# Linear attention and a gated MLP on one core: batch 1's q loaded ahead of its k and transposed by DMA, with two stages reordered around it

## The chip, the core and the metric

The kernel runs on one core of a Trainium2 chip. A core has a tensor engine (PE; its weight loads are listed apart as PEld), a vector engine (VectorE, DVE), a scalar engine (ScalarE, ACT), GpSimd (POOL) and a sync engine (SyncE, SP), which here only issues DMA transfers. All engines run their own lists of instructions in program order and wait for each other by semaphores. The core's 16 DMA engines move all transfers; those issued by GpSimd appear as queue q0 (software_dynamic), those issued by SyncE as queue q1 (hardware_dynamic). SBUF is the on-chip memory with 128 partitions, PSUM the small memory into which the tensor engine writes.

The metric is the device time of one execution in microseconds. Before the change its median is 295.08 us over 3 runs (294.52 to 295.19).

## The reference

Eight batches of eight heads, 576 positions, 64 values a head. Linear attention, then an MLP whose gate has a slope of its own for each of the 2048 inner features:

```python
def _attn_ref(q, k, v):                       # each (8, 8, 576, 64)
    def phi(x):
        return np.where(x > 0, x, np.exp(x) - 1.0) + 1.0
    q_p, k_p = (phi(q), phi(k))
    kv = np.einsum('bhsd,bhse->bhde', k_p, v)
    z = np.sum(k_p, axis=2)
    num = np.einsum('bhsd,bhde->bhse', q_p, kv)
    den = np.einsum('bhsd,bhd->bhs', q_p, z)[..., None] + 1e-06
    return num / den

def _moe_ref(x, w_in, w_out, beta):           # x (4608, 512), w_in (512, 2048), w_out (2048, 512)
    h = x @ w_in
    g = h * (1.0 / (1.0 + np.exp(-beta * h)))
    return g @ w_out
```

Between the two, the heads of a position are laid side by side, so that x has one row of 512 for each of the 4608 positions.

## The kernel before

The program is written in the order in which each engine is to run it; no scheduler moves anything. phi is computed as min(exp(x), max(x, 0) + 1): the exponential `e` on ScalarE, the rest on VectorE.

```python
def phi_all(b, a):                            # a is "q" or "k"; each in two halves pr of four heads
    phi_tile(b, a)
    for pr in range(2):
        phi_part(b, a, pr, xin(b, a, pr))     # e, ScalarE
    for pr in range(2):
        phi_relu(b, a, pr, xin(b, a, pr))     # r, VectorE
    for pr in range(2):
        phi_min(b, a, pr)                     # min(e, r), VectorE
```

The sums over k (`z_products`) and the products of k with v (`kv_direct`) are both chains of 36 small products for each half, with k as the stationary operand. `z_evac` and `kv_evac` bring them to SBUF and mask the parts that belong to other heads.

```python
def row_products(b, pr, dsts, mov):
    for j in range(J):                        # J = 9
        for hh in range(2):
            r = slice(hh * G, (hh + 1) * G)   # G = 64
            nc.tensor.matmul(dsts[hh], st[b, "k"][r, pr, j, :], mov(r, j),
                             start=(j == 0), stop=(j == J - 1), skip_group_check=True)
```

For the denominators (`dens`) and the numerators (`numer`, `numer0`) q must stand with its 64 values on the partitions. There are two ways to that. `q_trans` lets the tensor engine multiply by the identity, into PSUM, and copies from there (18 products and 5 copies a batch). `q_trans_dma` lets two DMA transfers do it, issued by SyncE, each for 64 rows:

```python
def q_trans_dma(b):
    st[b, "qTd"] = work.tile([P, 38, G], BF16, tag="qT", name="qTd")
    nc.gpsimd.memset(st[b, "qTd"][:, 36:37], 0.0)
    for hh in range(2):
        st[b, "qTd", "dma"] = nc.sync.dma_start_transpose(
            out=st[b, "qTd"][:, hh * 2 * J : (hh + 1) * 2 * J],
            in_=st[b, "q"][hh * G : (hh + 1) * G].rearrange("p a j c -> p (a j c)"),
        )

def q_stat(b, t, hh, pr, n):
    if (b, "qTd") in st:
        i = (hh * 2 + pr) * J + 2 * t
        return st[b, "qTd"][:, i : i + 2, :].rearrange("p j g -> p (j g)")
    return st[b, "qT"][:, t, pr, hh, 0:n]
```

Before the change batches 0 and 1 use `q_trans`, batches 2 to 7 `q_trans_dma`. From batch 3 on, the loads of the q and k after that wait until the transposition has landed (`hold`, with the reason "share of the queues").

The loads are issued by GpSimd in this order, and cast f32 to bf16 on the way (w_out alone stays f32):

```python
# k of batch 0, v of batch 0, w_in in four quarters, then
for i in range(3):
    load_w_out(i)
load(nc.gpsimd, xk[1], k, 1)
load(nc.gpsimd, xq[1], q, 1)
load_w_out(3)
load(nc.gpsimd, vb[1], v, 1)
# ... and, written after batch 0's h:
load(nc.gpsimd, xq[2], q, 2)
load(nc.gpsimd, xk[2], k, 2)
load(nc.gpsimd, vb[0], v, 2)
```

The front, batch 0 (`idle` puts products without use on the tensor engine, to keep its clock up):

```python
idle(3)
zt = [num0_tile() for _ in range(2)]
z_products(0, 0, zt)
idle(6)
z_products(0, 1, zt)
bps = miscps.tile([P, FC], F32, tag="misc", name="bps")
nc.tensor.matmul(bps, beta_row, ident16, is_transpose=True, start=True, stop=True)
nc.scalar.copy(beta_s, bps)
z_evac(zt)
# ...
kv_direct(0, 0, kvp0)
for hh in range(2):
    kv_evac(0, hh, (0,), kvp0)
dens(0, range(4), dps)
recips(0, 4, P, dps)
numer_part((0, 1), 0)                         # products and norm on VectorE
numer_part((2, 3), 0)
kv_direct(0, 1, kvp0)
# then x_part (transposes x, copy on ScalarE) and h0_part (pieces of h, first quarter of w_in)
```

Batch 0's y = g @ w_out, in four quarters of the inner features, with batch 1's attention between them. `y_mm(0, t, i, ...)` is four products of 512 columns, row group t, quarter i; `w_out_scale` divides a quarter of w_out by beta on VectorE, four instructions.

```python
for i in range(3):
    w_out_scale(i, 0)
yps = [mm_tile("y_ps") for _ in range(4)]
phi_all(1, "k")
phi_all(1, "q")
for i in range(2):
    for t in range(4):
        y_mm(0, t, i, yps[t])
kv1 = [miscps.tile([P, 512], F32, tag="misc", name="kv1") for _ in range(2)]
kv_tile(1)
y_mm(0, 0, 2, yps[0])
y_mm(0, 1, 2, yps[1])
for pr in range(2):
    z_products(1, pr, kv1)
z_evac(kv1)
w_out_scale(3, 0)
y_mm(0, 2, 2, yps[2])
for ts in ((0, 1), (2, 3)):
    q_trans(1, ts, num0_tile().bitcast(BF16), (nc.scalar, nc.scalar))
y_mm(0, 3, 2, yps[3])
dps1 = num0_tile()
q_trans(1, (4,), dps1.bitcast(BF16)[:, 512:768], (nc.scalar,))
for pr in range(2):
    kv_direct(1, pr, kv1)
for hh in range(2):
    kv_evac(1, hh, (0, 1), kv1)
dens(1, range(NT), dps1)                      # NT = 5
# recips, y_mm(0, 0, 3), numer0(1, 0), numer0(1, 1), then the rest of y, numer0 and x_trans in turn
```

Then follow, for batches 1 to 8 (8 is the remainder of all batches), `h_phase`, 16 steps of four products of 512 columns, and `y_phase`, 16 more, in which the next batches' attention is woven in at numbered steps (`at(sh, step, ...)`, `at(sy, step, ...)`). PSUM has two buffers for the transpositions of x (`miscps`).

Of the kernel before, what the change touches and what calls it, by code (L numbers as in the profile page):

```python
# [9 lines left out]
BF16 = mybir.dt.bfloat16  # L10
# [6 lines left out]
def kernel(  # L17
# [10 lines left out]
    nc = tc.nc  # L28
# [50 lines left out]
    def load(eng, dst, src, b, h0=0, n=4):  # L79

        rows = src[b].rearrange("h (g j) d -> (h g) (j d)", j=J)
        return eng.dma_start(  # L82
            out=dst[:, h0 : h0 + n].rearrange("p h j d -> p h (j d)"),
            in_=rows.rearrange("(i p) e -> p i e", p=P)[:, h0 : h0 + n],
        )
# [34 lines left out]
    def load_w_out(i):  # L120
        nc.gpsimd.dma_start(out=w_out_f[i], in_=w_out_v[:, i * 4 : (i + 1) * 4, :])
# [6 lines left out]
    def idle(n, cols=512):  # L128
        for _ in range(n):
            nc.tensor.matmul(  # L130
                warm_ps[:, 0:cols], warm[:, 0:P], warm[:, 0:cols], start=True, stop=True
            )
# [70 lines left out]
    def kv_direct(b, pr, ps):  # L203
        row_products(
            b, pr, [a[:, pr * P : (pr + 1) * P].rearrange("p (h d) -> p h d", h=2) for a in ps],
            lambda r, j: vb[b][r, 2 * pr : 2 * pr + 2, j, :],
        )

    def kv_evac(b, hh, prs, ps):
        p0, p1 = prs[0], prs[-1] + 1  # L210
        nc.vector.tensor_mul(
            st[b, "kv"][:, hh, p0:p1].rearrange("p a (h e) -> p a h e", h=2)[:, :, :, 0:D],
            ps[hh][:, p0 * P : p1 * P].rearrange("p (a h d) -> p a h d", a=p1 - p0, h=2),
            kvmask[:, p0:p1, :, 0:D],
        )
# [54 lines left out]
# [5 lines that stand above are left out]
# [68 lines left out]
    def mm_tile(name):  # L343
        return mmps.tile([P, 512], F32, tag="mm", name=name)

    def y_mm(b, t, i, yp, c0=0, c1=512):
        for c in range(4):
            ff = 4 * i + c
            nc.tensor.matmul(  # L349
                yp[:, c0:c1],  # L350
                g_sb[b % 2][:, ff, t * P : (t + 1) * P],
                w_out_sb[i][:, c, c0:c1],
                start=(ff == 0), stop=(ff == FC - 1), skip_group_check=True,
            )
# [22 lines left out]
    def phi_all(b, a):  # L377
        phi_tile(b, a)
        for pr in range(2):
            phi_part(b, a, pr, xin(b, a, pr))  # L380
        for pr in range(2):
            phi_relu(b, a, pr, xin(b, a, pr))
        for pr in range(2):
            phi_min(b, a, pr)
# [19 lines left out]
    def dens(b, ts, dps):  # L404

        for t in ts:
            n = P if t < NT - 1 else G
            for hh in range(2):
                for pr in range(2):
                    c = ((t * 2 + hh) * 2 + pr) * 2  # L410
                    nc.tensor.matmul(
                        dps[:n, c : c + 2], q_stat(b, t, hh, pr, n), z0[:, hh, pr, :],
                        start=True, stop=True, skip_group_check=True,
                    )

# [5 lines left out]
    def num0_tile():  # L421
        return num0ps.tile([P, 512], F32, tag="num0", name="nps0")

    def numer0(b, t):
        n = P if t < NT - 1 else G
        nps = num0_tile()
        for hh in range(2):
            for pr in range(2):
                nc.tensor.matmul(  # L429
                    nps[:n, (hh * 2 + pr) * P : (hh * 2 + pr + 1) * P].rearrange(  # L430
                        "p (h d) -> p h d", h=2
                    ),
                    q_stat(b, t, hh, pr, n),
                    st[b, "kv"][:, hh, pr, :].rearrange("p (h e) -> p h e", h=2)[:, :, 0:D],
                    start=True, stop=True, skip_group_check=True,
                )
        norm(b, t, n, nps[:n].rearrange("p (a h d) -> p a h d", a=2, h=4), rden0[:n, t])
# [14 lines left out]
    phi_step("q", 1, phi_relu)  # L452
    for i in range(3):
        load_w_out(i)
    load(nc.gpsimd, xk[1], k, 1)
    load(nc.gpsimd, xq[1], q, 1)
    load_w_out(3)
    load(nc.gpsimd, vb[1], v, 1)
    phi_step("q", 1, phi_min, 0, 4)
# [15 lines left out]
    idle(3)  # L475
    zt = [num0_tile() for _ in range(2)]
    z_products(0, 0, zt)
    idle(6)
    z_products(0, 1, zt)
    bps = miscps.tile([P, FC], F32, tag="misc", name="bps")  # L480
    nc.tensor.matmul(bps, beta_row, ident16, is_transpose=True, start=True, stop=True)
# [4 lines left out]
        q_trans(0, (t,), misc_bf()[:, 0 : 512 if t < NT - 1 else 256], (nc.scalar,))  # L486

    def numer_part(ts, pr):

        nps = num0_tile()  # L490
        for i, t in enumerate(ts):
            for hh in range(2):
                nc.tensor.matmul(  # L493
                    nps[:, (i * 2 + hh) * P : (i * 2 + hh + 1) * P].rearrange(
                        "p (h d) -> p h d", h=2
                    ),
                    q_stat(0, t, hh, pr, P),
                    st[0, "kv"][:, hh, pr, :].rearrange("p (h e) -> p h e", h=2)[:, :, 0:D],
                    start=True, stop=True, skip_group_check=True,
                )  # L500
        for i, t in enumerate(ts):
            if pr == 0:
                st[0, "xs", t] = work.tile([P, 4, 2, D], BF16, tag="xs", name="xs", bufs=4)
            nc.vector.tensor_mul(
                st[0, "xs", t][:, 2 * pr : 2 * pr + 2].rearrange("p i a d -> p a i d"),
                nps[:, i * 256 : (i + 1) * 256].rearrange("p (a h d) -> p a h d", a=2, h=2),
                rden0[:, t, :, 2 * pr : 2 * pr + 2, None].to_broadcast([P, 2, 2, D]),
            )
# [20 lines left out]
                    skip_group_check=True,  # L529
                )  # L530

    kv_direct(0, 0, kvp0)
    for hh in range(2):
        kv_evac(0, hh, (0,), kvp0)
    dens(0, range(4), dps)
    recips(0, 4, P, dps)
    numer_part((0, 1), 0)
    numer_part((2, 3), 0)
    kv_direct(0, 1, kvp0)

# [65 lines left out]
    for i in range(3):  # L606
        w_out_scale(i, 0)
    yps = [mm_tile("y_ps") for _ in range(4)]
    phi_all(1, "k")
    phi_all(1, "q")  # L610
    for i in range(2):
        for t in range(4):
            y_mm(0, t, i, yps[t])
    kv1 = [miscps.tile([P, 512], F32, tag="misc", name="kv1") for _ in range(2)]
    kv_tile(1)
    y_mm(0, 0, 2, yps[0])
    y_mm(0, 1, 2, yps[1])
    for pr in range(2):
        z_products(1, pr, kv1)
    z_evac(kv1)  # L620
    w_out_scale(3, 0)
    y_mm(0, 2, 2, yps[2])
    for ts in ((0, 1), (2, 3)):
        q_trans(1, ts, num0_tile().bitcast(BF16), (nc.scalar, nc.scalar))
    y_mm(0, 3, 2, yps[3])
    dps1 = num0_tile()
    q_trans(1, (4,), dps1.bitcast(BF16)[:, 512:768], (nc.scalar,))
    for pr in range(2):
        kv_direct(1, pr, kv1)
    for hh in range(2):  # L630
        kv_evac(1, hh, (0, 1), kv1)
    dens(1, range(NT), dps1)
    recips(0, 4, P, dps1)
    recips(4, 5, G, dps1)
    y_mm(0, 0, 3, yps[0])
    y_out(0, 0, yps[0], copier=nc.scalar)
    numer0(1, 0)
    numer0(1, 1)
    phi_tile(2, "q")
    phi_tile(2, "k")  # L640
    phi_part(2, "q", 0, xin(2, "q", 0))
    y_mm(0, 1, 3, yps[1])
    x_trans(1, 0, nc.scalar)
    numer0(1, 2)
    phi_part(2, "q", 1, xin(2, "q", 1))
    y_mm(0, 2, 3, yps[2], 0, 256)
    x_trans(1, 1, nc.vector)
    numer0(1, 3)
    y_mm(0, 2, 3, yps[2], 256, 512)
    y_mm(0, 3, 3, yps[3], 0, 256)  # L650
    x_trans(1, 2, nc.vector)
    y_mm(0, 3, 3, yps[3], 256, 512)
    x_trans(1, 3, nc.vector)
    phi_part(2, "k", 0, xin(2, "k", 0))
    y_out(0, 1, yps[1], copier=nc.scalar)
    phi_part(2, "k", 1, xin(2, "k", 1))
    for t in (2, 3):
        y_out(0, t, yps[t])
# [42 lines left out]
    for b in range(1, B + 1):  # L701
        n = b + 1
        sh, sy = {}, {}
        if b == 1:
            at(sh, 0, lambda: q_trans_dma(2))
            at(sh, 8, lambda: x_trans(1, 4, nc.vector))
            at(sh, 1, lambda: [v_copy(nc.gpsimd, 2, pr) for pr in range(2)])
            at(sh, 2, lambda: load_kq(3, st[2, "qTd", "dma"]), lambda: load_v(3))
        if n < B:
            at(sh, 6 if b == 1 else 4, lambda: kv_both(n))  # L710
            for t in range(NT):
                ff = (8 if b == 1 else 5) + 2 * t
                for g, f in ((ff, numer), (ff + 1, x_trans_dma)):
                    at(*((sh, g) if g < FC else (sy, g - FC)), lambda t=t, f=f: f(n, t))
        if n + 1 < B:
            m = n + 1
            at(sy, 0, lambda: phi_all(m, "q"))
            at(sy, 2, lambda: q_trans_dma(m), lambda: load_kq(m + 1, st[m, "qTd", "dma"]))
            at(sy, 6, lambda: phi_all(m, "k"), lambda: [v_copy(nc.gpsimd, m, pr) for pr in range(2)])
            at(sy, 7, lambda: load_v(m + 1))  # L720
        h_phase(b, xT[b % 3] if b < B else xT_tail, sh)
        y_phase(b, sy, last=(b == B))
# [30 lines left out]
```

## Time and profile before

Shares are of the profiled span of 293.1 us; the mean granted clock of the tensor engine is 0.997.

| engine | busy us | share of the span |
|---|---|---|
| tensor engine (PE) | 284.6 | 97% |
| ScalarE | 160.0 | 55% |
| VectorE | 116.2 | 40% |
| GpSimd | 36.9 | 13% |

| DMA transfer | issues | us from issue to landing (median) |
|---|---|---|
| transposition of q (up to 80 us) | 4 | 4.5 |
| loads of q by GpSimd (up to 80 us) | 3 | 21.4 |
| transposition of xs (up to 80 us) | 4 | 8.1 |

In the lines of the profile, `L349` is a line of the kernel, `y_ps<-w_out,g` names what is written and what is read, `x36` is a count. A timeline line begins with start and duration in us; in its brackets stand the idle time just ahead of it and what ended it. A piece of the chain of work that ended last has start, duration and work; pieces follow one another to the end of the span, so a gap in the tensor engine shows up there as a piece of another engine. A line of a DMA queue gives packets, MB and the time of the packets as a share of 16 engines' window. That share can go over 100%, since a DMA engine has several packets under way.

### The profile page before, as it was taken

The page shows a single profiled execution, that of the slowest core. Times are in us where ns is not written, and L with a number is a line of the kernel's source. Part 1 is how long each engine was busy: PE and PEld are TensorE (multiplying, and loading weights), DVE is VectorE, ACT ScalarE, POOL GpSimd, SP SyncE. Part 2 cuts the span into 40 slices and gives each one's busy share as a digit, 9 for nine tenths or more (in the row PEclk, how much of TensorE's full clock was granted, in tenths as well). Part 3 has the DMA queues.
Part 4 walks back from the last instruction along what each step waited for, and adds up shares of the span by engine and source line. Part 5 has one row for each costly group of instructions (what it writes and reads, how often), then busy time and mean ns, then how long its engine had stood idle before and what let it go on. Part 6 is the DMA issues. An engine that isn't in the chain of part 4 may idle for free.

```text
span 293.1 us, 4762 instructions
## 1 busy us (share of the span) xinstructions
PE 284.6 (97%) x1885; PEld 143.0 (49%) x1885; DVE 116.2 (40%) x267; ACT 160.0 (55%) x217; POOL 36.9 (13%) x54
## 2 busy tenths in 40 slices
PE   7899999999999999999999999999999999999994
PEld 2574457455445444544454445544554444444443
DVE  5742776943905361446135613562251200110021
ACT  5677857957545863677257815790660077017500
POOL 8632100320050005000500043000000000000000
PEclk9999999999999999999999999999999999999998
DMA  7999999699699769964997399838132310130033
GB/s 218 204 225 387 259 234 182 136 224 187 95 173 281 128 71 225 261 76 59 189 284 97 47 198 264 111 46 154 38 72 45 74 36 0 44 84 17 0 72 75
DMA packets 50887, 40.83 MB, mean 139 GB/s; under 512 B 30752, under 2 KB 42288, under 8 KB 50864
## 3 DMA queue, kind: packets, MB, share of 16 engines
q1 hardware_dynamic: 37968, 23.48, 38.7%
q0 software_dynamic: 12736, 16.91, 29.7%
q8 instruction: 15, 0.25, 0.3%
q10 hardware_dynamic: 160, 0.13, 0.2%
q14 instruction: 8, 0.07, 0.1%
HBM read 36.71 MB, written 9.44 MB: 157 GB/s over the span
## 4 chain that ended last, share of the span: by engine, by line
PE 93%; DMA 4%; ACT 1%; DVE 1%; issue 0%; SPq 0%; POOLq 0%
PE y_ps L349 43%; PE h_ps L331 40%; PE nps L282 2%; DMA xk<-in_k_dram 2%; PE kvp L176 2%; DMA qTd<-phi_q 2%; PE h_ps L524 1%; PE kv L187 1%; PE warm_ps L130 0%; PE nps L429 0%; PE kvp L187 0%; ACT e L141 0%; PE xtp L312 0%; PE nps L493 0%; PE nps L254 0%
## 5 line engine op out<-in xcount | busy, mean ns | idle before, releaser
L339 ACT ACTIVATE g<-h_ps,beta_c 128x512 bf16<-128x512 f32 x144 | 98.0, 688 | 101.4 <-PE h_ps L331 100.9
L349 PE MATMUL y_ps<-w_out,g 128*128 128x512 bf16 (+3 forms) x600 | 127.2, 371 | 0.0
L331 PE MATMUL h_ps<-xT,w_in 128*128 128x512 bf16 x496 | 114.7, 379 | 0.3 <-DVE xT L319 0.2
L349 PEld LDWEIGHTS <-g 128*128 128x128 bf16 x600 | 58.1, 98 | 64.9
L331 PEld LDWEIGHTS <-w_in 128*128 128x128 bf16 x560 | 52.7, 97 | 57.8 <-issue 0.2
L234 DVE COPY y_sb<-y_ps 128x512 f32<-128x512 f32 (+2 forms) x35 | 23.4, 673 | 84.7 <-PE y_ps L349 81.0
L296 DVE TENSOR_TENSOR xs<-nps,rden 128x512 bf16<-128x512 f32 (+1 forms) x36 | 24.7, 689 | 5.9 <-DMA xT<-xs 3.4
L82 POOL DMA_DIRECT2D xq<-in_q_dram x7 | 5.2, 744 | 109.2 <-DMA qTd<-phi_q 105.6
L141 ACT ACTIVATE e<-xk 128x1152 bf16<-128x1152 bf16 x16 | 17.9, 1153 | 1.4 <-DMA xk<-in_k_dram 1.3
L152 DVE TENSOR_TENSOR phi_q<-e,r 128x1152 bf16<-128x1152 bf16 (+2 forms) x17 | 12.0, 721 | 14.0 <-ACT e L141 13.7
L141 ACT ACTIVATE e<-xq 128x1152 bf16<-128x1152 bf16 x14 | 15.6, 1155 | 0.1
L331 PE MATMUL h_ps<-xT_tail,w_in 128*128 128x512 bf16 x64 | 14.0, 379 | 0.0
L226 DVE TENSOR_TENSOR kv_bd<-kvp,kvmask 128x260 bf16<-128x260 f32 x12 | 4.6, 424 | 23.7 <-PE kvp L176 23.7
L290 DVE TENSOR_SCALAR den<-nps 128x8 f32<-128x8 f32 (+1 forms) x30 | 4.9, 165 | 22.7 <-PE nps L282 22.7
L282 PEld LDWEIGHTS <-qTd 128*128 128x128 bf16 x120 | 9.3, 98 | 7.4 <-DMA qTd<-phi_q 0.5
L152 DVE TENSOR_TENSOR phi_k<-e,r 128x1152 bf16<-128x1152 bf16 x16 | 11.6, 753 | 2.3 <-ACT e L141 2.0
L282 PE MATMUL nps<-kv_bd,qTd 128*128 128x130 bf16 x120 | 12.1, 221 | 0.3 <-DMA qTd<-phi_q 0.3
L166 POOL CAST vaug<-vf 128x1152 bf16<-128x1152 f32 x10 | 11.2, 1157 | 2.3 <-DMA vf<-in_v_dram 2.3
L130 PE MATMUL warm_ps<-xT 128*128 128x512 bf16 x24 | 7.4, 465 | 1.5 <-DVE xT L95 1.5
L141 ACT ACT_TABLE_LOAD x6 | 7.7, 1283 | 1.4 <-DMA xk<-in_k_dram 0.7
L339 ACT ACT_TABLE_LOAD x6 | 7.7, 1283 | 0.1
L176 PEld LDWEIGHTS <-phi_k 64*128 64x128 bf16 x216 | 6.3, 94 | 2.5 <-issue 2.1
(81 smaller groups left out, 121.8 us busy)
## 6 DMA issues: line engine op xcount, KB each, us to landing
out_dram<-y_sb SPq DMA_DIRECT2D x70, 128.0 KB, 2.4
vf<-in_v_dram SPq DMA_DIRECT2D x5, 1152.0 KB, 8.4
xk<-in_k_dram POOLq DMA_DIRECT2D x7, 576.0 KB, 13.8
xq<-in_q_dram POOLq DMA_DIRECT2D x7, 576.0 KB, 9.6
w_in<-in_moe_w_in_dram POOLq DMA_DIRECT2D x4, 512.0 KB, 12.5
g<-in_moe_w_out_dram POOLq DMA_DIRECT2D x2, 1024.0 KB, 17.9
stage<-in_moe_w_out_dram POOLq DMA_DIRECT2D x2, 1024.0 KB, 20.3
stage<-in_q_dram SPq DMA_DIRECT2D x2, 576.0 KB, 4.1
```

The costliest lines, as they stand in the source:

```text
L82: return eng.dma_start(out=dst[:, h0 : h0 + n].rearrange("p h j d -> p h (j d)"), in_=rows.rearrange("(i p) e -> p i e", p=P)[:, h0 : h0 + n],
L130: nc.tensor.matmul(warm_ps[:, 0:cols], warm[:, 0:P], warm[:, 0:cols], start=True, stop=True)
L141: nc.scalar.activation(st[b, a, pr, "e"][:, :, j0:j1], x[:, :, j0:j1], ACTF.Exp)
L152: nc.vector.tensor_tensor(st[b, a][:, pr, j0:j1].rearrange("p j (h d) -> p j h d", h=2), st[b, a, pr, "e"][:, :, j0:j1].rearrange("p h j d ...
L166: eng.tensor_copy(vaug[b % 2][:, pr, :, :, 0:D], src[:, 2 * pr : 2 * pr + 2].rearrange("p h j d -> p j h d"),)
L176: nc.tensor.matmul(ps[hh, pr], st[b, "k"][r, pr, j, :], vaug[b % 2][r, pr, j, :, 0:EA], start=(j == 0), stop=(j == J - 1), skip_group_chec ...
L234: eng.tensor_copy(dst, src)
L282: nc.tensor.matmul(nps[: qs.shape[-1], hh, pr * 2 * EA : (pr + 1) * 2 * EA], qs, st[b, "kv"][:, hh, pr, :], start=True, stop=True, skip_gr ...
L296: nc.vector.tensor_mul(xs[:n].rearrange("p i a d -> p a i d"), num, rd[:, :, :, None].to_broadcast([n, 2, 4, D]),)
L331: nc.tensor.matmul(hp[:, c0:c1], w_in_sb[ff // 4][:, kc, (ff % 4) * P : (ff % 4 + 1) * P], x[:, kc, c0:c1], start=(kc == 0), stop=(kc == K ...
L339: nc.scalar.activation(g_sb[b % 2][:, ff, :], hp, ACTF.Silu, scale=beta_c[:, ff : ff + 1])
L349: nc.tensor.matmul(yp[:, c0:c1], g_sb[b % 2][:, ff, t * P : (t + 1) * P], w_out_sb[i][:, c, c0:c1], start=(ff == 0), stop=(ff == FC - 1), ...
```

## The change

It gives batch 1's q to the DMA transposition, as batches 2 to 7 have it. So that q is ready in time, q is loaded and put through phi ahead of k, and three quarters of batch 0's y stand in one run where the transpositions stood between them. The denominators of batch 1 now come ahead of its products of k with v. In the front, the products of batch 0's first half of k and v come ahead of the second sums, in place of four of the fillers, and the first numerators ahead of the denominators. In the loop, two steps of batch 2 and two of batch 3 come somewhat later.

```diff
             for hh in range(2):
                 for pr in range(2):
                     c = ((t * 2 + hh) * 2 + pr) * 2
+                    qs = q_stat(b, t, hh, pr, n)
                     nc.tensor.matmul(
-                        dps[:n, c : c + 2], q_stat(b, t, hh, pr, n), z0[:, hh, pr, :],
+                        dps[: qs.shape[-1], c : c + 2], qs, z0[:, hh, pr, :],
                         start=True, stop=True, skip_group_check=True,
                     )
# ... numer0 likewise ...
-    load(nc.gpsimd, xk[1], k, 1)
     load(nc.gpsimd, xq[1], q, 1)
+    load(nc.gpsimd, xk[1], k, 1)
     load_w_out(3)
# ...
     z_products(0, 0, zt)
-    idle(6)
+    idle(2)
+    kv_direct(0, 0, kvp0)
+    for hh in range(2):
+        kv_evac(0, hh, (0,), kvp0)
     z_products(0, 1, zt)
# ... numer_part is split into numer_mm (products) and numer_norm (VectorE) ...
-    kv_direct(0, 0, kvp0)
-    for hh in range(2):
-        kv_evac(0, hh, (0,), kvp0)
+    nps_a = numer_mm((0, 1), 0)
     dens(0, range(4), dps)
     recips(0, 4, P, dps)
-    numer_part((0, 1), 0)
+    numer_norm((0, 1), 0, nps_a)
     numer_part((2, 3), 0)
     kv_direct(0, 1, kvp0)
# ...
+    phi_all(1, "q")
+    q_trans_dma(1)
     phi_all(1, "k")
-    phi_all(1, "q")
-    for i in range(2):
+    for i in range(3):
         for t in range(4):
             y_mm(0, t, i, yps[t])
     kv1 = [miscps.tile([P, 512], F32, tag="misc", name="kv1") for _ in range(2)]
     kv_tile(1)
-    y_mm(0, 0, 2, yps[0])
-    y_mm(0, 1, 2, yps[1])
     for pr in range(2):
         z_products(1, pr, kv1)
     z_evac(kv1)
     w_out_scale(3, 0)
-    y_mm(0, 2, 2, yps[2])
-    for ts in ((0, 1), (2, 3)):
-        q_trans(1, ts, num0_tile().bitcast(BF16), (nc.scalar, nc.scalar))
-    y_mm(0, 3, 2, yps[3])
+    y_mm(0, 0, 3, yps[0])
+    y_out(0, 0, yps[0], copier=nc.scalar)
     dps1 = num0_tile()
-    q_trans(1, (4,), dps1.bitcast(BF16)[:, 512:768], (nc.scalar,))
+    dens(1, range(NT), dps1)
+    recips(0, 4, P, dps1)
+    recips(4, 5, G, dps1)
     for pr in range(2):
         kv_direct(1, pr, kv1)
     for hh in range(2):
         kv_evac(1, hh, (0, 1), kv1)
-    dens(1, range(NT), dps1)
-    recips(0, 4, P, dps1)
-    recips(4, 5, G, dps1)
-    y_mm(0, 0, 3, yps[0])
-    y_out(0, 0, yps[0], copier=nc.scalar)
+    y_mm(0, 1, 3, yps[1])
+    y_out(0, 1, yps[1], copier=nc.scalar)
     numer0(1, 0)
     numer0(1, 1)
# ... the rest of y's last quarter follows one group later; x_trans(1, 1) is now
#     copied by ScalarE instead of VectorE, and y_out(0, 1) no longer stands at the end ...
# in the loop:
-                ff = (8 if b == 1 else 5) + 2 * t
+                ff = (9 if b == 1 else 5) + 2 * t
# ...
-            at(sy, 0, lambda: phi_all(m, "q"))
-            at(sy, 2, lambda: q_trans_dma(m), lambda: load_kq(m + 1, st[m, "qTd", "dma"]))
+            late = 2 if b == 1 else 0
+            at(sy, late, lambda: phi_all(m, "q"))
+            at(sy, 2 + late, lambda: q_trans_dma(m), lambda: load_kq(m + 1, st[m, "qTd", "dma"]))
```

More of the change, by code (lines that the diff above doesn't have):

```diff
@@ L428, in numer0 @@
             for pr in range(2):
+                qs = q_stat(b, t, hh, pr, n)
                 nc.tensor.matmul(
-                    nps[:n, (hh * 2 + pr) * P : (hh * 2 + pr + 1) * P].rearrange(
+                    nps[: qs.shape[-1], (hh * 2 + pr) * P : (hh * 2 + pr + 1) * P].rearrange(
                         "p (h d) -> p h d", h=2
                     ),
-                    q_stat(b, t, hh, pr, n),
+                    qs,
                     st[b, "kv"][:, hh, pr, :].rearrange("p (h e) -> p h e", h=2)[:, :, 0:D],
@@ L454 @@
         load_w_out(i)
+    load(nc.gpsimd, xq[1], q, 1)
     load(nc.gpsimd, xk[1], k, 1)
-    load(nc.gpsimd, xq[1], q, 1)
     load_w_out(3)
@@ L488, in numer_part, with numer_mm @@
     def numer_part(ts, pr):
+        numer_norm(ts, pr, numer_mm(ts, pr))
+    def numer_mm(ts, pr):
         nps = num0_tile()
@@ L500, in numer_part, with numer_norm @@
                 )
+        return nps
+    def numer_norm(ts, pr, nps):
         for i, t in enumerate(ts):
@@ L641 @@
     phi_part(2, "q", 0, xin(2, "q", 0))
-    y_mm(0, 1, 3, yps[1])
+    y_mm(0, 2, 3, yps[2])
     x_trans(1, 0, nc.scalar)
@@ L645 @@
     phi_part(2, "q", 1, xin(2, "q", 1))
-    y_mm(0, 2, 3, yps[2], 0, 256)
-    x_trans(1, 1, nc.vector)
+    y_mm(0, 3, 3, yps[3], 0, 256)
+    x_trans(1, 1, nc.scalar)
     numer0(1, 3)
-    y_mm(0, 2, 3, yps[2], 256, 512)
-    y_mm(0, 3, 3, yps[3], 0, 256)
+    y_mm(0, 3, 3, yps[3], 256, 512)
     x_trans(1, 2, nc.vector)
-    y_mm(0, 3, 3, yps[3], 256, 512)
     x_trans(1, 3, nc.vector)
     phi_part(2, "k", 0, xin(2, "k", 0))
-    y_out(0, 1, yps[1], copier=nc.scalar)
     phi_part(2, "k", 1, xin(2, "k", 1))
```

## The prediction

> **What bounds the kernel now.** I read the page first, then the chain of work that ended last in order of time, then the timelines of VectorE and of the DMA issuer around batch 1, and last the DMA queues in three windows.
>
> ```profile
> span 293.1 us, 4762 instructions
> PE 284.6 (97%) x1885; PEld 143.0 (49%) x1885; DVE 116.2 (40%) x267; ACT 160.0 (55%) x217; POOL 36.9 (13%) x54
> PE 93%; DMA 4%; ACT 1%; DVE 1%; issue 0%; SPq 0%; POOLq 0%
> ```
>
> The tensor engine is the bound: it is busy 97% of the span and makes up 93% of the chain. Every instruction taken from it inside the chain is a gain of its own duration, and every new wait put in front of it is a loss of the whole wait, since nothing else runs there in its place. The chain of batch 1's stage, in order of time (start, duration, what):
>
> ```profile
> 41.18 0.54 PE kv L187 x36
> ...
> 42.69 0.90 PE nps L254 x16
> ...
> 44.45 0.12 PE nps L254 x2
> 44.57 1.11 PE kv L187 x36
> 45.68 0.70 PE nps L411 x20
> 46.38 0.97 PE y_ps L349 x4
> ```
>
> L254 is the transposition of q, L187 the sums over k and the products of k with v, L411 the denominators. Here there is no gap at all between 41.18 and 51.8.
>
> VectorE's timeline shows when phi of k and q is ready, and when the last quarter of w_out has been scaled:
>
> ```profile
> 33.93 0.83 DVE L145 TENSOR_SCALAR r<-xk 128x1152 bf16<-128x1152 bf16 x2 [0.30 <-DMA xk<-in_k_dram]
> 36.47 0.76 DVE L152 TENSOR_TENSOR phi_k<-e,r 128x1152 bf16<-128x1152 bf16 x1 [1.70 <-ACT e L141]
> 37.52 0.76 DVE L152 TENSOR_TENSOR phi_k<-e,r 128x1152 bf16<-128x1152 bf16 x1 [0.29 <-ACT e L141]
> ...
> 41.90 1.67 DVE L597 TENSOR_SCALAR w_out<-stage,rbeta 128x512 bf16<-128x512 f32 x4
> ```
>
> The first of batch 1's two inputs lands at 33.93, and its phi is complete at 37.52 + 0.76 = 38.28. This landing is set by the load queue, so it does not move with the tensor engine.
>
> The same DMA transposition that the change adds for batch 1 exists for batch 2, and can be read there. First the issue, and its time in the chain:
>
> ```profile
> 55.98 3.62 SPq L265 DMA_TRANSPOSE qTd<-phi_q  x2
> ```
>
> ```profile
> 57.44 4.75 DMA qTd<-phi_q
> 62.19 0.05 issue
> 62.24 0.29 PE nps L282 x2
> ```
>
> From issue to the use of the result: 62.24 - 55.98 = 6.3 us, of which 57.44 - 55.98 = 1.5 us lie ahead of the transfer. The DMA queues in the window 57.3 to 61.8 show that these transfers had the engines to themselves:
>
> ```profile
> q1 hardware_dynamic: 2364, 0.60, 98.2%
> ```
>
> About 2304 packets (2 x 64 rows x 18 blocks) of 256 B, 2364 with the neighbours', fill 16 engines for 4.3 us: some 2304 / 4.3 = 535 packets a us. The window 39.8 to 51.5, where batch 1's transposition would fall, looks different:
>
> ```profile
> q0 software_dynamic: 1717, 1.90, 95.4%
> ```
>
> That is the rest of GpSimd's loads (v of batch 1, then q, k and v of batch 2), 1717 packets, and they alone keep the engines busy.
>
> **What the Trainium skill says.** "DMA: Bandwidth & Descriptors", section "Queues, rings and completion order": each DMA engine takes turns between the queues that have work for it, one packet from each. The same page, "Issuing engines are not separate DMA queues": transfers share the same 16 engines whoever issues them. The trace agrees. In the window 68.5 to 71.5 transpositions of xs stand beside loads of q and k:
>
> ```profile
> q0 software_dynamic: 407, 0.45, 93.4%
> q1 hardware_dynamic: 399, 0.10, 30.4%
> ```
>
> In 3.0 us, 136 load packets and 133 transposing packets a us: one for one, so a small 256 B packet waits for a large load packet each time. "TensorE: Matmul & The Clock Gate", "Part 1: The HAM clock gate", says that about 3.4 us of idleness halve the clock and that about 3.4 us of work restore it. The trace agrees with the second half:
>
> ```profile
> 1.46 4.46 PE L130 MATMUL warm_ps<-xT 128*128 128x512 bf16 x12 [1.46 <-DVE xT L95]
> ```
>
> The first eight of these fillers start 0.43 us apart, up to 4.8 us; from 5.1 us on it is 0.215. No wait in this trace is long enough to show the first half.
>
> **The change part by part.**
>
> *The front (10 to 20 us).* Four of six fillers go, 4 x 0.23 = 0.93 us (the row of six took 1.40), and kv_direct (0.61) takes their place ahead of the second sums. Its v should land about 11.0: the packets of k's second half ended near 8.2 and its exponential started at 9.60, so 1.4 us later, and v's first half ended at 9.65. From 11.06 (10.59 + 2 x 0.23) kv_direct runs to 11.7, the sums to about 12.05, and the first numerators (0.33) cover VectorE's masking of the sums. The second kv_direct ends at 14.0 instead of 14.86. But the first piece of h needs the first quarter of w_in, and GpSimd, which waits for that load, goes on at 15.3. So h starts at 15.3 instead of 15.72, a gain of 0.4 us.
>
> *Batch 1's transpositions.* 18 go from the tensor engine: 0.90 + 0.12 = 1.02 us, all in the chain. Five copies on ScalarE (2.33 us) go too, beside the path.
>
> *Y0's three quarters in one run.* This only reorders products; it holds the tensor engine busy to 42.9 + 0.54 - 0.4 = 43.05. The scaling of w_out's last quarter (four of 0.42 us) still follows the sums on VectorE, but now only one group of products stands behind it, where before 4 us of other work did. That group ends near 45.2 instead of 43.9: 1.3 us lost, were nothing else in the way.
>
> *The DMA transposition.* q's phi is ready at 38.28, the issue follows, the first packet at 38.3 + 1.5 = 39.8. From there the 1717 load packets at 136 a us last 12.6 us, to 52.4. In that time the transposition gets 12.6 x 133 = 1680 of its 2304 packets. The remaining 624 at 535 a us take 1.2 us, to 53.6, and 0.5 us pass from the last packet to the use (61.7 to 62.2 in batch 2). The denominators, which need both halves, start at 54.1. Alone they could have started at 44.6, or at 45.2 after the scaling. The tensor engine stands idle for about 9 us.
>
> *From there to batch 1's h.* Warm, the rows of before: denominators 0.70, kv_direct 1.11, two and two half groups of y 0.86 + 0.86 + 0.44 + 0.43, four numerators 0.93, three transpositions of x 0.66: 6.0 us; then the last transposition, its copy and the start of h, 0.22 + 0.43 + 0.06: 6.7. ScalarE now has to copy both x_trans(1, 0) and x_trans(1, 1) between two exponentials of 1.16 us, and only two PSUM buffers serve these transpositions: I take 0.8 us for that. After 9 us of idleness the clock should be at half: 3.4 us of work at double time, 1.6 us more. Together 9.1, so h starts at 63.2 instead of 52.30: 10.9 us later. The front's 0.4 and the 1.02 us are inside this, not on top of it: the landing, not the tensor engine, sets the time.
>
> *The later shifts.* Batch 2's numerators a step later remove the wait ahead of 62.24, 0.3 us. Batch 3's phi and transposition move 1.7 us later; they landed 7 us ahead of their use (at 89.76) and stay hidden. Sum: +10.9 - 0.3 = +10.6, on 295.08: 305.7. As the clock and the copies may cost less than I took, I put 305.0.
>
> **The rivals.**
> - *The transposition is hidden.* If it took 6.3 us as in batch 2, it would land at 44.6 and the change would be worth 0.4 + 1.02 + 0.3, less 1.3 for the scaling and 0.8 for ScalarE: near 295.5. Y0's longer run is plainly laid out for this. Against it: the load queue is never empty from 39.8 to 49.5, and the one-for-one sharing is measured.
> - *The transposition is slowed, but less.* If its packets had two turns to one of a load's, a turn would cost 107 + 2 x 30 ns (load and transposing packets in the trace), 16 x 2 / 0.167 = 190 packets a us: 12 us, landing at 52.5. Even at four to one (227 ns, 280 a us) it is 8.2 us, landing at 48.5: then about 299.5. So the sign hangs little on the exact sharing.
> - *The clock stays up.* Then 1.6 us less: 304.
> - *The landing of the loads moves later too*, batch 2's k and v by 3 to 4 us. They are used after the wait, which is longer, so I expect no second wait.
>
> **Range and chances.** Shared one for one, with or without the clock: 303 to 307. Better sharing: 299 to 303. Hidden: 294 to 296.5, which I give about one chance in eight. 299 to 309 should hold the time 8 times in 10. Slower by over 2% means over 301.0: 0.83. Within 2%: 0.14. Faster by over 2% (below 289.2) would need more than twice all removed work: 0.03.
>
> **What would show it.** In the changed kernel's waits, the tensor engine's denominators (L412) wait 8 to 10 us for the DMA of qTd, from about 45 to 54, and no other wait is over 1 us. The DMA's time to landing for batch 1's qTd is near 14 us, batch 2's still 4 to 5. In 40 to 52 us both queues show about equal packets. The front's h starts near 15.3. The matmuls just after the wait are about twice as slow. It is wrong if the denominators' wait is under 2 us: then the transposing packets do not take turns with the loads here. It is wrong in size if the clock stays full after the wait, or if x_trans(1, 3) waits for no copy.

## The result and the profile after

The changed kernel takes 307.89 us (median, 307.36 to 309.82) beside 294.87 of the kernel before in the same runs: a ratio of 1.0454 with a 95% interval of 1.0407 to 1.0501. It is slower by 13 us. The page of the changed kernel:

```profile
span 305.6 us, 4682 instructions
PE 283.9 (93%) x1830; PEld 142.8 (47%) x1859; DVE 115.4 (38%) x266; ACT 158.3 (52%) x213; POOL 36.9 (12%) x55
PEclk9999995599999999999999999999999999999999
```

The tensor engine's share falls from 97% to 93%, so it has new gaps, and two of the 40 slices, at 46 to 61 us, show half its clock. The waits of the tensor engine, longest first (engine and line, for whom, us in total, how often, the longest):

```profile
PE nps L412 <- DMA qTd<-phi_q: 10.0, 2, 9.3
...
PE kvp L176 <- POOL vaug L166: 1.3, 2, 0.9
...
PE y_ps L349 <- DVE w_out L606: 0.7, 1, 0.7
PE xtp L312 <- ACT xT L317: 0.4, 1, 0.4
```

Nearly all of it is the denominators of batch 1 (L412), which wait for the DMA transposition. The second line is a wait that was not there before, in batch 2's stage. The tensor engine around the first, in order of time (start, duration, what, and in brackets the idle time ahead):

```profile
42.84 1.56 PE L349 MATMUL y_ps<-w_out,g 128*128 128x512 bf16 x4 [0.71 <-DVE w_out L606]
53.67 0.21 PE L412 MATMUL nps<-z,qTd 128*128 128x2 bf16 x2 [9.26 <-DMA qTd<-phi_q]
54.66 0.64 PE L412 MATMUL nps<-z,qTd 128*128 128x2 bf16 x18 [0.78 <-DMA qTd<-phi_q]
55.23 2.10 PE L187 MATMUL kv<-vf,phi_k 64*128 64x128 bf16 x36
```

The two waits are the two transfers, one for each 64 rows of q. They land at 53.67 and 54.66. The last line is the second thing to see: the 36 products of k and v (18 for each half) take 2.10 us here. In the timeline of before they took 1.18 (1.11 in its chain, where a piece ends with the start of the next):

```profile
44.50 1.18 PE L187 MATMUL kv<-vf,phi_k 64*128 64x128 bf16 x36
```

The issue, in the timeline of SyncE:

```profile
38.51 10.04 SPq L265 DMA_TRANSPOSE qTd<-phi_q  x2
```

Batch 2's pair took the issuer 3.62 us; this one holds it 10.04. And the two DMA queues in the window 46 to 51:

```profile
q0 software_dynamic: 714, 0.80, 92.3%
q1 hardware_dynamic: 728, 0.19, 27.7%
```

714 load packets and 728 transposing packets in 5 us: one for one, 143 and 146 a us.

Where the time goes, by the first product of each stage in the timelines:

| stage begins | before us | after us | difference |
|---|---|---|---|
| h of batch 0, whole rows | 20.81 | 19.50 | -1.31 |
| y of batch 0 | 32.39 | 31.07 | -1.32 |
| h of batch 1 | 52.30 | 64.24 | +11.94 |
| y of batch 1 | 69.11 | 80.58 | +11.47 |
| h of batch 2 | 83.15 | 94.62 | +11.47 |
| y of batch 2 | 99.40 | 112.38 | +12.98 |
| last y | 274.89 | 287.87 | +12.98 |

Three things happen: the stage of batch 1's attention loses 13.3 us, batch 2's numerators a step later win 0.47, and batch 2's h loses 1.5.

### The profile page after: what moved, and what is told of

It reads as the page before. It is cut to its first block, busy times and chain, and to the rows that moved or that the text cites. A ratio compares the mean times of both kernels' runs of the same rounds, so it can differ in the third digit from the quotient of the medians.

```text
span 305.6 us, 4682 instructions
## 1 busy us (share of the span) xinstructions
PE 283.9 (93%) x1830; PEld 142.8 (47%) x1859; DVE 115.4 (38%) x266; ACT 158.3 (52%) x213; POOL 36.9 (12%) x55
## 4 chain that ended last, share of the span: by engine, by line
PE 65%; DMA 2%; issue 1%; POOL 1%; DVE 1%; SPq 1%; POOLq 0%; DVEq 0%
PE y_ps L349 32%; PE h_ps L331 30%; PE nps L282 2%; PE kvp L176 2%; DMA qTd<-phi_q 2%; POOL vaug L166 1%; SPq L265 0%; DVE y_sb L234 0%; DVE phi_q L152 0%; DVE r L145 0%; SPq L364 0%; POOL xq L82 0%; POOLq L82 0%; POOL xk L82 0%; POOLq L263 0%
## 5 line engine op out<-in xcount | busy, mean ns | idle before, releaser
L331 PE MATMUL h_ps<-xT,w_in 128*128 128x512 bf16 x480 | 112.9, 379 | 0.9 <-DVE xT L319 0.3
L152 DVE TENSOR_TENSOR phi_q<-e,r 128x1152 bf16<-128x1152 bf16 (+2 forms) x17 | 12.1, 720 | 15.6 <-ACT e L141 15.3
L232 ACT COPY y_sb<-y_ps 128x512 f32<-128x512 f32 x2 | 1.2, 585 | 18.8 <-PE y_ps L349 18.8
L412 PE MATMUL nps<-z,qTd 128*128 128x2 bf16 x20 | 0.8, 167 | 10.0 <-DMA qTd<-phi_q 10.0
L176 PE MATMUL kvp<-vaug,phi_k 64*128 64x130 bf16 x216 | 7.5, 217 | 1.3 <-POOL vaug L166 1.3
```

The costliest lines, as they stand in the source:

```text
L152: nc.vector.tensor_tensor(st[b, a][:, pr, j0:j1].rearrange("p j (h d) -> p j h d", h=2), st[b, a, pr, "e"][:, :, j0:j1].rearrange("p h j d ...
L176: nc.tensor.matmul(ps[hh, pr], st[b, "k"][r, pr, j, :], vaug[b % 2][r, pr, j, :, 0:EA], start=(j == 0), stop=(j == J - 1), skip_group_chec ...
L331: nc.tensor.matmul(hp[:, c0:c1], w_in_sb[ff // 4][:, kc, (ff % 4) * P : (ff % 4 + 1) * P], x[:, kc, c0:c1], start=(kc == 0), stop=(kc == K ...
```

## The experiments

The theory to be tested is that the transposition is late because its small packets take turns with GpSimd's loads. The rivals are that it is slow by itself, or that the new order costs the time. Each diff is against the kernel named.

### All loads of batch 2 held (e1)

```diff
 # the changed kernel
-    load(nc.gpsimd, xq[2], q, 2)
-    load(nc.gpsimd, xk[2], k, 2)
-    load(nc.gpsimd, vb[0], v, 2)
 ...
     phi_all(1, "q")
     q_trans_dma(1)
+    hold(load(nc.gpsimd, xq[2], q, 2), st[1, "qTd", "dma"])
+    load(nc.gpsimd, xk[2], k, 2)
+    load(nc.gpsimd, vb[0], v, 2)
```

> The three loads of batch 2 (q, k, v) start only when batch 1's transposition has landed. Theory (one-for-one sharing with the loads): the transposition has the DMA engines nearly to itself, lands about 6.3 us after its issue, near 45, and the denominators wait 1 us at most. The held q of batch 2 then lands near 51, and since ScalarE takes its exponential ahead of the copies of x, a wait of 2 to 4 us appears there: h of batch 1 near 55 to 57, 297 to 300 us in all. Rival (the transposition is slow by itself here, by its issue or its source, whatever else the DMA engines do): the denominators still wait 8 us or more, 307 to 309 us or above.

Measured: 300.28 us, ratio to before 1.0179 (1.0132 to 1.0226), 0.3 above the expected band. The tensor engine's timeline:

```profile
44.81 0.20 PE L412 MATMUL nps<-z,qTd 128*128 128x2 bf16 x2 [0.49 <-DMA qTd<-phi_q]
45.72 0.62 PE L412 MATMUL nps<-z,qTd 128*128 128x2 bf16 x18 [0.70 <-DMA qTd<-phi_q]
46.27 2.10 PE L187 MATMUL kv<-vf,phi_k 64*128 64x128 bf16 x36
```

The same transposition, issued at the same time (38.4), lands 9 us earlier. So it is the loads that delay it; "slow by itself" falls. The price shows up in ScalarE's timeline:

```profile
52.53 1.16 ACT L141 ACTIVATE e<-xq 128x1152 bf16<-128x1152 bf16 x1 [2.10 <-DMA xq<-in_q_dram]
```

The held q of batch 2 lands at 52.5, and the copies of x stand behind its exponential; the tensor engine waits 2.5 us for them. Of the 9 us some 7.6 are kept. The clock is at half here too (the products of k and v again take 2.10), though no single wait is over 0.71 us: from 42.0 to 45.7 the tensor engine waits 0.71, 0.49 and 0.70 us, 1.9 in three pieces. It is at half once more from about 56.1 to 59.5, behind the waits for ScalarE's copies.

### Only the last load held (e2)

```diff
 # the changed kernel
-    load(nc.gpsimd, vb[0], v, 2)
 ...
     q_trans_dma(1)
+    hold(load(nc.gpsimd, vb[0], v, 2), st[1, "qTd", "dma"])
```

> Only the last of the three loads (batch 2's v, 512 packets) waits for the transposition; q and k of batch 2 stay beside it. Theory: one third of the competing packets is gone, some 1200 are left from 39.8 on; at 136 a us they end 8.9 us later, 1180 transposing packets have gone by then, the other 1120 take 2.1 us: landing about 51.3 instead of 54, so the wait shrinks by 2.5 to 3 us and the time is about 305. Rival (slow by itself): wait and time as in the changed kernel, 307.9.

Measured: 304.66 us, ratio 1.0317 (1.0263 to 1.0371). The landings are at 50.73 and 51.68 (expected 51.3), 2.9 and 3.0 us earlier; the tensor engine's waits:

```profile
PE nps L412 <- DMA qTd<-phi_q: 6.6, 2, 5.9
```

One of three competing loads taken away gives 3 of the 9 us, three give all. The landing follows the number of competing packets, as turns of one for one have it.

### The tensor engine transposes again, all else as changed (e3)

```diff
 # the changed kernel
-    q_trans_dma(1)
 ...
+    for ts in ((0, 1), (2, 3)):
+        q_trans(1, ts, num0_tile().bitcast(BF16), (nc.scalar, nc.scalar))
     y_mm(0, 0, 3, yps[0])
-    y_out(0, 0, yps[0], copier=nc.scalar)
     dps1 = num0_tile()
+    q_trans(1, (4,), dps1.bitcast(BF16)[:, 512:768], (nc.scalar,))
+    y_out(0, 0, yps[0], copier=nc.scalar)
```

> Batch 1's q is transposed by the tensor engine again (18 products, 5 copies by ScalarE), everything else of the change stays: q ahead of k, three quarters of y in one run, the new front, the later steps of batches 2 and 3. Theory: the 10 us of waiting and the halved clock go; the front's gain (0.7 to 1.3) and 0.4 at batch 2's numerators stay, the 1.5 lost in batch 3 stays: 294.5 to 296.5 us. Rival (the new order itself costs the time): over 300 us.

Measured: 296.77 us, ratio 1.0075 (1.0056 to 1.0094). The median lies 0.3 above the expected band, but far below 300: the new order costs little, the DMA transposition most. By stages, from h of batch 0 (19.65) to h of batch 1 (52.75) are 33.10 us, beside 31.49 before. So the new order by itself loses 1.6 us of the 13.3 in this stage, among them 0.6 of waiting for ScalarE's copy of the last transposition and 0.4 for its copy of x; the DMA transposition makes up the rest. In the total the earlier front hides this loss: h of batch 2 begins at 83.13, as before. Then y of batch 2 begins at 100.98, 1.6 later than before. That remainder is the next experiment's.

### Batch 3's steps as before (e4)

```diff
 # the changed kernel
-            late = 2 if b == 1 else 0
+            late = 0
```

> Batch 3's phi and transposition of q at their old steps 0 and 2 of batch 1's y, all else as changed. Theory: the later step delays the loads of batch 4, which wait for that transposition at the head of GpSimd's list, and with them the copies of batch 3's v behind them; undone, the wait of the products of k and v for those copies (1.3 us) goes: 306.3 to 306.7 us. Rival (that wait comes from the shifted landing of v, not from GpSimd's order): 307.9 as changed.

Measured: 306.19 us, ratio 1.0377 (1.0318 to 1.0436), 1.7 below the changed kernel and 0.1 below the expected band. Batch 2's h takes 16.36 us again (94.76 to 111.12), as before (16.25), instead of 17.76. Why it costs is seen in GpSimd's timeline of the changed kernel:

```profile
97.31 0.74 POOL L82 DMA_DIRECT2D xq<-in_q_dram  x1 [20.96 <-ACT g L339]
98.04 0.75 POOL L82 DMA_DIRECT2D xk<-in_k_dram  x1
98.77 2.25 POOL L166 CAST vaug<-vf 128x1152 bf16<-128x1152 f32 x2
```

The bracket names one of several waits. The load is held until batch 3's transposition has landed, which in the chain is at 91.92 + 4.83 = 96.75:

```profile
91.92 4.83 DMA qTd<-phi_q
```

The copies of batch 3's v stand behind the two loads in GpSimd's list. Their products (L176) wait for each half of the copy:

```profile
99.99 0.70 PE L176 MATMUL kvp<-vaug,phi_k 64*128 64x130 bf16 x18 [0.89 <-POOL vaug L166]
101.08 0.70 PE L176 MATMUL kvp<-vaug,phi_k 64*128 64x130 bf16 x18 [0.39 <-POOL vaug L166]
```

With the old steps the loads go out at 96.00 instead of 97.31, the copies begin at 97.46, and the 36 products run without a break. The transposition itself was in time in both.

### Fillers in the wait (e5)

```diff
 # the changed kernel
     y_out(0, 0, yps[0], copier=nc.scalar)
+    warm_ps = num0_tile()
+    idle(40)
     dps1 = num0_tile()
```

> The changed kernel with 40 products without use (8.6 us) on the tensor engine between the first group of y's last quarter and the denominators, so that it is busy while it waits. Theory (the landing sets the end of the wait, and the idleness halves the clock after it): the denominators still start near 54.7 with a wait of 1 to 2 us left, and what follows runs at full clock: the products of k and v take 1.1 instead of 2.1 us, and 2 to 2.5 us are saved in all, 305.4 to 306.2 us. Rival (the clock costs nothing, or the fillers' end sets the time): 307.5 or above.

Measured: 305.03 us, ratio 1.0362 (1.0342 to 1.0381), 2.9 below the changed kernel and 0.4 below the expected band. The landing is the same (54.76), but now:

```profile
55.29 1.18 PE L187 MATMUL kv<-vf,phi_k 64*128 64x128 bf16 x36
```

From the landing to batch 1's h are 7.34 us (54.76 to 62.10) instead of 9.58 (54.66 to 64.24). So the halved clock after the wait costs 2.2 us there; 0.5 of the rest comes from a shorter wait for the copies of v.

### The transposition at its best (e8)

```diff
 # e1, with late = 0
+    w_out_scale(3, 0)
     for pr in range(2):
         z_products(1, pr, kv1)
     z_evac(kv1)
-    w_out_scale(3, 0)
     y_mm(0, 0, 3, yps[0])
     y_out(0, 0, yps[0], copier=nc.scalar)
+    # kv_direct(1) and kv_evac(1), y_mm(0, 1, 3) and y_out(0, 1)
     dps1 = num0_tile()
     dens(1, range(NT), dps1)
 # ... and batch 2's exponentials behind the copies of x
```

> The DMA transposition at its best: the three loads of batch 2 wait for it, the products of k and v and a second group of y stand ahead of the denominators, w_out's last quarter is scaled ahead of the masking of the sums, ScalarE copies x ahead of batch 2's exponentials, batch 3's steps as before. Theory: the denominators wait 0.5 us at most, but the held loads land near 52 (q) and 55 (k), the exponentials and so the change to the gate's table come late, and the tensor engine stops after four groups of batch 1's h until ScalarE takes them: 3 to 5 us lost there, 296 to 299 us. Rival (a hidden transposition is worth the work that it removes): 292.5 to 293.5 us.

Measured: 300.92 us, ratio 1.0225 (1.0207 to 1.0242), above both bands. The denominators wait 0.7 us only, and h of batch 1 begins at 51.34, 0.96 earlier than before. But then, in the tensor engine's timeline,

```profile
51.34 3.61 PE L331 MATMUL h_ps<-xT,w_in 128*128 128x512 bf16 x15 [0.28 <-DVE xT L319]
60.48 4.26 PE L331 MATMUL h_ps<-xT,w_in 128*128 128x512 bf16 x12 [5.53 <-ACT g L339]
```

and in ScalarE's:

```profile
52.39 2.22 ACT L141 ACTIVATE e<-xq 128x1152 bf16<-128x1152 bf16 x2 [2.36 <-DMA xq<-in_q_dram]
56.22 2.22 ACT L141 ACTIVATE e<-xk 128x1152 bf16<-128x1152 bf16 x2 [1.61 <-DMA xk<-in_k_dram]
```

ScalarE waits for the held loads before it can turn to the gate, and once four PSUM tiles of h are full, the tensor engine stands for 5.5 us. The wait has not gone, it has moved from the transposition to what was held for it. The mechanism was as expected; its size was not: 5.5 us where 3 to 5 were expected, and a time 2 us over the band. Behind the wait the clock is at half again (0.58 from 60 to 61, 0.50 from 61 to 63), so that batch 1's h takes 23.5 us (51.34 to 74.88) instead of 16.8.

### The front alone, and its fillers (e6, e7, e9, e10)

e6 is the kernel before with the new front, e7 the same with batch 2's numerators one step later (9 for 8).

> The kernel before with the new front alone: kv_direct of the first half ahead of the second sums in place of four fillers, and the first numerators ahead of the denominators. Theory: h starts when the first quarter of w_in has landed, 0.4 to 1.3 us earlier, and the tensor engine passes this on to the end: 293.3 to 294.2 us beside 294.6. Rival (the gain is taken back by the later landing of w_out or of batch 1's k): 294.6.

> As the run before, and batch 2's numerators one step later (9 instead of 8), with batch 3's steps left as they were. Theory: the wait of 0.3 us for batch 2's transposition goes too, and since batch 3's loads are not delayed nothing is lost later: 0.3 to 0.45 us below the front alone, 292.9 to 293.8 us, the best of all. Rival: no difference to the front alone.

Measured: e6 295.41 us, ratio 1.0026 (1.0014 to 1.0039); e7 295.10, ratio 1.0023 (1.0006 to 1.0040). Both miss: the front alone is no gain, rather a small loss. For e6 the engines' busy time in stretches shows part of the reason (after the stretch: sum and busy us of each engine, then the granted clock, DMA share and GB/s):

```profile
12.00:14.00 2.00, 1.78 (x39) 1.59 (x41) 1.14 (x7) 1.25 (x3) 1.10 (x2) 0.78 1.25 206
14.00:16.00 2.00, 1.63 (x21) 1.26 (x18) 1.17 (x4) 1.41 (x6) 0.72 (x1) 0.50 1.24 210
```

The clock is at half from about 13 to 16.5 us. In the timed executions the mean clock of e6 was below 0.995 in 8 of 16, with a median of 295.7 us, and 295.1 in the others; of e7 in 6 of 22, 296.7 and 294.6; of the kernel before in none of the 37 beside them. The fillers had a use. The clock is not all of it: in the executions where it holds, e6 is still at 295.1 beside 294.69 of before, and no trace here shows what takes the front's gain in those. Where e7's clock holds, another wait takes it: 1.0 us within batch 2's h, at 85.31, for a copy of y on VectorE that a store holds up. Beside e6 the median of e7 is 0.3 lower, as was expected of the later step; but the two spread widely (294.56 to 296.59 and 293.46 to 297.12), so that this gain is not shown.

e9 puts fillers where the tensor engine waits anyway, e10 takes only fillers away:

```diff
 # e9: e6, and                                  # e10: the kernel before, and
-    idle(3)                                    -    idle(6)
+    idle(5)                                    +    idle(2)
     z_products(0, 0, zt)
 ...
     z_evac(zt)
+    idle(1)
 ...
     kv_direct(0, 1, kvp0)
+    idle(1)
```

> The new front alone, with four products without use put back where the tensor engine waits anyway: two more ahead of the first sums, one after the second sums, one after the second products of k and v. Theory (the front alone gained nothing because with four fillers fewer the clock falls to half near 12 us in some executions): the mean granted clock is again 0.996 or more in every run, h starts 0.6 to 1.1 us earlier than before, 293.5 to 294.1 us beside 294.7. Rival (the reordered front has no gain to give, the clock aside): 294.7 or above.

> The kernel before with two fillers instead of six ahead of the second sums, nothing else. Theory (the removed fillers let the clock fall): no gain, clocks of 0.985 to 0.995 in some executions, 294.8 to 296 us with a wider spread than before. Rival (fillers were only time on the tensor engine): at most as before, 294.0 to 294.7, with clocks of 0.996 and more.

Measured: e9 294.46 us, ratio 0.9995 (0.9984 to 1.0006), its clock 0.997 or more in all 14 executions; e10 294.97, ratio 1.0025 (1.0010 to 1.0040), its clock below 0.99 in 6 of 22 with a median of 296.8, and 294.8 in the others. The clock's part is as expected. The gain is not: e9 was expected at 293.5 to 294.1, and its interval includes a ratio of 1. In e9 h of batch 1 begins at 51.00, 1.3 earlier than in the profile of before, but y of batch 1 only 0.46 earlier, mostly since batch 2's numerators now wait 0.8 us for their transposition (0.3 before). Some of the 1.3 is not the front's either: in the profile of before batch 0's k came 0.7 us later than in those of e9 and the changed kernel (its exponential starts at 8.20 beside 7.44 and 7.54), and e10, without the new front, begins its h at 19.79, only 0.28 after e9.

### What is left of the change (e11)

```diff
 # e9, and
-                ff = (8 if b == 1 else 5) + 2 * t
+                ff = (9 if b == 1 else 5) + 2 * t
 ...
+            late = 2 if b == 1 else 0             # batch 3's phi of q and its transposition
+            # and for b == 1 the copies of v at step 2, ahead of the held loads, not at step 6
```

> The new front with the fillers put back (e9), batch 2's numerators one step later, batch 3's phi and transposition of q two steps later as in the change, but GpSimd copies batch 3's v ahead of the loads that wait for that transposition instead of behind them. Theory: neither the wait for batch 2's transposition (0.8 us in e9) nor the one for the copies of v (1.3 us in the changed kernel) nor that for a copy of y (1.0 us in e7) is left, so the front's 1.3 us reach the end: 293.2 to 293.9 us beside 294.7. Rival (another wait takes their place): 294.3 or above.

Measured: 293.79 us, ratio to before 0.9972 (0.9961 to 0.9983): faster than before by 0.9 us and than the changed kernel by 14. The tensor engine has no wait over 0.2 us left after the first 8 us:

```profile
PE warm_ps L130 <- DVE xT L95: 1.5, 1, 1.5
PE tp L254 <- DVE phi_q L152: 0.4, 1, 0.4
PE h_ps L331 <- DVE xT L319: 0.2, 1, 0.2
```

So the front and the later steps together are worth 0.3%, with the fillers put back and with the copies of v moved. The front's share of it is not shown: the later steps and the moved copies were not run without it. In none of the arrangements run here is the DMA transposition of batch 1 worth having.

## Why the prediction was right, and where it was not

- *The transposition lands late because it shares the DMA engines one for one.* Right: 53.67 and 54.66 measured, 54.1 predicted; e1 and e2 show the cause. On the way two terms were off and cancelled. The first packet came not 1.5 but some 4 us after the issue (at 38.51; the transposing queue has no packet from 38 to 42 and 70 from 42 to 43), and the loads, alone for that long, were nearly done earlier: 138 of their packets go from 50 to 51, 73 in the next microsecond and 18 in the one after it, where they had been put to last at the full rate to 52.4. That the landing came within 0.6 us is in part luck.
- *The tensor engine stands about 9 us, then runs at half clock.* Right in kind: 10.0 us of waiting. The clock was put at 1.6 us and costs 2.2 (e5): it stayed at half until about 60.0, 5.3 us after the wait for q ended, where 3.4 us of work had been assumed. h of batch 1 was predicted at 63.2 and begins at 64.24.
- *Scaling and ScalarE's copies.* The scaling was put at 1.3 us, measured 0.71; the copies at 0.8, measured 0.42.
- *The front, 0.4 us.* It begins 1.3 us earlier in the profile, part of it from an earlier landing of batch 0's k. Its first piece did wait for the first quarter of w_in, as predicted (0.17 us), but started at 14.39 and not at 15.3. In the changed kernel this did not matter, since the landing of q sets the time. What I overlooked is that the four removed fillers kept the clock up.
- *Batch 2's numerators, -0.3 us.* Measured -0.47.
- *Batch 3 "landed 7 us ahead of their use and stay hidden".* This step failed. The transposition did stay hidden, but what stands behind it in GpSimd's list did not: 1.5 us (e4). I had followed the shifted transfer to its own use, and not the loads held for it nor the copies of v behind those. With the 1.0 us by which batch 1's h begins later than predicted (0.6 of it the clock), less 0.2 at batch 2's numerators, and with the 0.7 that I had taken off the sum of 305.7, this makes 3.0 us; 2.9 lie between 305.0 and 307.89. The time is inside the wide range of 299 to 309, but 0.9 above the 303 to 307 given for one-for-one sharing.
- *The rival "hidden", near 295.5.* It was thought of as a transposition with free DMA engines at no cost. e8 has it nearly hidden and takes 300.92: there the engines were freed by holding loads that batch 2 needs at once. Whether some other order frees them at less cost was not run.

## What to carry to other kernels

Before moving work from a full engine to the DMA, count the packets that stand in the other queues at that very time: a transfer of many small packets beside one of large ones takes as many turns as it has packets, here 14.6 us from issue to landing, beside 6.0 in e1 with three loads held. If a hold is put in a list of instructions, look at everything behind it in the same list when what it waits for moves. Work without use that keeps a clock up is part of the design, and is to be replaced when it is removed.

## What the runs showed of the hardware that was not expected

- Beside queued loads a DMA transposition was held up at its issue too: the first packet about 4 us after it instead of 1.5, and the pair held SyncE's list for 10.04 us instead of 3.62 (4.88 in e1, with the loads held). What delays the first packet is not shown. A store issued behind it waits as well: its data was ready at 45.02, and it goes out at 48.59.
- The tensor engine's clock fell to half with no single wait over 0.71 us (e1). "TensorE: Matmul & The Clock Gate" of the Trainium skill, in "Part 1: The HAM clock gate", puts the fall after at least one idle window of about 3.4 us, and tells also of a kernel whose short pauses between groups of products were enough; in this run short waits among small products were enough.
- The time from the last product to the fall of the clock was not the same from run to run: about 1.9 us in the changed kernel (44.40 to 46.3), 3.0 in e2 (44.83 to 47.8) and 5.2 in e8 (54.95 to 60.2), worked out from the granted clock of the one-microsecond stretch in which it falls (0.65, 0.92 and 0.58).
